# Keys of two batches loaded in packets of 768 bytes and turned in seven overlapping pieces per pair of heads

## The chip, the core and the metric

The kernel runs on one core of a Trainium2 chip. Its metric is the device time of one execution in microseconds (us). Three executions of the kernel before took 891.18, 894.32 and 895.53 us, so the median is 894.32 us. TensorE (PE) multiplies matrices and also turns (transposes) tiles by multiplying them with an identity matrix; its weight loads are listed apart as PEld. VectorE (DVE), ScalarE (ACT) and GpSimd (POOL) work on elements. SyncE (SP) issues most of the transfers (DMA) between the device's memory and the on-chip memory.

## The reference

Four batches of attention with twelve heads, 448 positions and 64 elements per head, with one 12x12 mix of the heads before the softmax and one after it, and behind it a gated feed-forward layer:

```python
scores = scale * np.matmul(q, k.transpose(0, 1, 3, 2))
scores = np.einsum('bhij,hg->bgij', scores, w_pre)
scores = scores - np.max(scores, axis=-1, keepdims=True)
attn = np.exp(scores)
attn = attn / (np.sum(attn, axis=-1, keepdims=True) + 1e-09)
attn = np.einsum('bhij,hg->bgij', attn, w_post)
attn_out = np.matmul(attn, v)
x = attn_out.transpose(0, 2, 1, 3).reshape(B * S, H * D)     # 1792 x 768
g = x @ w_gate                                                # 768 x 1536
out = (g / (1 + np.exp(-g)) * (x @ w_val)) @ w_out
```

## The kernel before

The work is a list of steps, each with a key (a number that says when it stands in the program). The steps are sorted by key and written out once, and each engine runs its own instructions in that order. Nothing is scheduled again on the chip: an instruction that waits holds up all that stands behind it on its engine, SP's transfers included.

Per batch, `load_k` brings the keys of a pair of heads. The first 384 positions are spread so that partition p holds positions 3p, 3p+1 and 3p+2. `load_k` puts the tile's columns in the order (position, head, element): three groups of 128 columns, each with 64 elements of the first head and 64 of the second. The 64 elements of one position and one head are a run of 256 bytes at both ends. The last 64 positions of all heads come in a transfer of their own (line 192 for batch 0, line 202 for the others). Batch 0's keys lie in one tile, and its loads are issued by SP and ACT in turn; batch 1 has a tile per pair, loaded by SP while batch 0 is computed.

`kprep` (line 228) turns a pair: three pieces of 128x128 and one for the last 64 positions (64x128) go to one bank of PE's output memory (`ktr`), and `kcopy` (lines 234 and 236) copies the bank to `kk`, with 64 partitions for each head. `qprep` and `qcopy` (lines 245, 252) do the same to the queries. `qk` (line 275) multiplies queries and keys, `qkcopy` (lines 284, 286) copies the scores to `stg`, and `store` (line 294) sends them to memory (`s_all`). `gather` (line 305) brings them back with positions and heads on the partitions (`rs`), `pre` (line 324) mixes the heads, `top` (335), `expo` (341) and `norm` (348 to 352) make the softmax, `post` (368) mixes again and turns, `mixed` (383) copies, and `av` (410) multiplies with the values (`vn`, loaded in lines 170 and 176). The feed-forward layer comes after batch 3, from about 400 us on.

At the start the order on PE is: 28 turns of the identity (line 218), queries, keys of pairs 0 and 1, queries, keys of pair 2, the first group of scores (`qk_0_0`, pairs 0 and 1), keys of pairs 3, 4 and 5, and the second and third group of scores. SP stores a group of scores, loads queries and values, stores the second and the third group, loads more values, and issues the first gathers. Batch 1's keys are turned one pair at a time between the `qk` and the `post` of one round of batch 0, from 65 to 89 us.

Of the kernel before, what the change touches and what calls it, by code (L numbers as in the profile page):

```python
# [24 lines left out]
def talking_heads_moe_kernel(ctx, tc, q, k, v, w_pre, w_post, w_gate, w_val, w_out, out):  # L25
    nc = tc.nc
    B, H, S, D = q.shape
    NT, DM = out.shape
    DFF = w_out.shape[0]
    P = 128  # L30
    TS = 10
    NC = -(-S // P)
    PART = S % P
# [64 lines left out]
    ident = cst.tile([P, P], F32, name="ident")  # L98
# [53 lines left out]
    qn, kn, vn, kk, qt, stg, rs, pts, sts, et, rw, ats, trs, qtrs, qks = ({} for _ in range(15))  # L152


    def keys(c):
        return min(P, S - c * P)
# [28 lines left out]
    def load_k(b, p, part=None, eng=nc.sync):  # L185
        full = S - PART
        n = (NC - 1) * 2 * D
        if b == 0:
            if "all" not in kn:
                kn["all"] = stp.tile([P, NPAIR * NC * 2 * D], F32, tag="stg", name="kn_0")  # L190
            if part == 1:
                eng.dma_start(
                    out=kn["all"][:PART, NPAIR * n:].rearrange("p (h d) -> p h d", d=D),
                    in_=k[b, :, full:].rearrange("h p d -> p h d"),
                )
                return
            t = kn["all"][:, p * n:(p + 1) * n]
            last = kn["all"][:PART, NPAIR * n + p * 2 * D:NPAIR * n + (p + 1) * 2 * D]
        else:
            if p == 0:  # L200
                kn["last"] = nat.tile([PART, H, D], F32, tag="kl", name=f"kl_{b}")
                nc.sync.dma_start(out=kn["last"], in_=k[b, :, full:].rearrange("h p d -> p h d"))
            t = nat.tile([P, n], F32, tag="kn", name=f"kn_{b}_{p}", bufs=6)
            last = kn["last"][:, 2 * p:2 * p + 2].rearrange("p h d -> p (h d)")
        eng.dma_start(
            out=t.rearrange("p (c j d) -> p (c j) d", j=2, d=D),
            in_=k[b, 2 * p:2 * p + 2, :full].rearrange("j (p c) d -> p c j d", c=NC - 1),
        )
        kn[b, p] = [t[:, c * 2 * D:(c + 1) * 2 * D] for c in range(NC - 1)] + [last]

    def first_act():
        t = smp.tile([P, 1], F32, tag="st", name="first_act", bufs=4)
# [7 lines left out]
    def kprep(b, p):  # L220
        kt = kn.pop((b, p))
        if b == 0:
            tr = ps.tile([P, S], F32, tag="pre" if p in (2, 3) else "post", name=f"ktr_{b}_{p}")
        else:
            tr = ps.tile([P, S], F32, tag="tr", bufs=2, name=f"ktr_{b}_{p}")
        for c in range(NC):
            m = keys(c)
            nc.tensor.transpose(tr[:, c * P:c * P + m], kt[c], ident[:m, :m])
        trs[b, p] = tr

    def kcopy(b, p):
# [234 lines left out]
    for b in range(B):  # L466
# [7 lines left out]
        if b == 0:  # L474
            at(-61.0, later(load_q, b, 0, nc.scalar))
            at(-60.9, first_act)
            at(-61.0, later(load_k, b, 0))
            at(-60.9, later(load_k, b, None, 1))
            for p in range(1, NPAIR):
                at(-60.8 + 0.01 * p, later(load_k, b, p, 0, nc.scalar if p % 2 else nc.sync))  # L480
# [3 lines left out]
            for i, (what, *a) in enumerate(order):  # L484
                n = -40.0 + i
                if what == "q":
                    at(n, later(qprep, b, *a))
                    at(n + 0.2, later(qcopy, b, *a))
                elif what == "k":
                    at(n, later(kprep, b, *a))  # L490
                    at(n + 0.2, later(kcopy, b, *a))
                else:
                    at(n, later(qk, b, *a))
                    for x in range(2):
                        at(n + 0.1, later(qkcopy, b, *a, x))
                    if a[0] == 0:
                        at(n + 0.6, later(store, b, *a, (nc.sync, nc.scalar)))
                    else:
                        at(n + 1.6, later(store, b, *a, (nc.sync, nc.scalar)))
        else:  # L500
            for p in range(NPAIR):
                n = slot(BACK - NUB - 4 + p)
                at(n0 - NTB + 0.4 + 0.01 * p if b > 1 and p < 3 else n - (9.3 if b > 1 else 4), later(load_k, b, p))
                at(n + 0.65, later(kprep, b, p))
                at(n + 0.8, later(kcopy, b, p))
# [396 lines left out]
    def gap(i, act=False):  # L902
        return (B - 1) * NTB + i // 2 * 2 + ((1.0, 1.84) if act else (0.7, 1.95))[i % 2]
# [4 lines left out]
    for b in range(NT // TB):  # L908
# [15 lines left out]
        for i in range(NFC):  # L924
            f = i // 2 + i % 2 * NFH if b else i
            n = n0 + i * T_F[b]
            if b:
# [19 lines left out]
                else:  # L947
                    last = f == NFC - 1
# [16 lines left out]
        if b:  # L965
            for i, (x, more, bq) in enumerate(AO):
                n = DOWN + i * NTC * T_Q
                for j in range(NFH // 2):
                    at_ff(n - 10.9 + 0.1 * j if i == 0 else n - 16 + j, later(b_load, i, j))
                    y, z = ((-6.6, -5.6), (-4.9, -3.9), (-1.6, -0.6))[j] if i == 0 else (3 * j - 12, 3 * j - 11)  # L970
                    at_ff(n + y, later(b_split, i, j, False))
                    at_ff(n + z, later(b_split, i, j, True))
                for c in range(NTC):
                    m = n + c * T_Q
# [25 lines left out]
        for n, u in units:  # L1000
            if unit_index(u) < EARLY:
# [4 lines left out]
                last = gap(FIRST + 5 * i + 5)  # L1006
# [13 lines left out]
            else:  # L1020
                d = n - LEAD
# [62 lines left out]
```

## Time and profile before

| what | value |
|---|---|
| median of three executions | 894.32 us (891.18 to 895.53) |
| the profiled execution, its own time | 898.02 us |
| its span, first to last instruction | 896.3 us |
| PE busy (matmuls) | 855.8 us, 95% of the span |
| DVE busy | 641.5 us, 72% |
| ACT busy | 457.9 us, 51% |
| DMA queue that SP issues to (q1) | 71.6% of 16 engines' span |

The profiled execution took 1.7 us more than its span and 3.7 us more than the median. An engine's busy time is an average over parts with different limits: from 400 us on PE has hardly a gap, while in the first 90 us it shares the time with transfers that keep all DMA engines busy. A row of the timeline gives start and length in us, the engine (a q behind it means that its sequencer issued a transfer), the line, the operation, output<-input, the shape and the count of instructions that were merged; in brackets stand the idle time of the engine ahead of the row and what ended it. "Issue" there means that the engine waited for nothing that the profile shows. A form such as 128*64 says rows * columns of the weights that PE holds; here that is the tile to be turned.

### The profile page before, as it was taken

The page shows a single profiled execution, that of the slowest core. Times are in us where ns is not written, and L with a number is a line of the kernel's source. Part 1 is how long each engine was busy: PE and PEld are TensorE (multiplying, and loading weights), DVE is VectorE, ACT ScalarE, POOL GpSimd, SP SyncE. Part 2 cuts the span into 40 slices and gives each one's busy share as a digit, 9 for nine tenths or more (in the row PEclk, how much of TensorE's full clock was granted, in tenths as well). Part 3 has the DMA queues.
Part 4 walks back from the last instruction along what each step waited for, and adds up shares of the span by engine and source line. Part 5 has one row for each costly group of instructions (what it writes and reads, how often), then busy time and mean ns, then how long its engine had stood idle before and what let it go on. Part 6 is the DMA issues. An engine that isn't in the chain of part 4 may idle for free.

```text
span 896.3 us, 26474 instructions
## 1 busy us (share of the span) xinstructions
PE 855.8 (95%) x10886; PEld 704.5 (79%) x10886; DVE 641.5 (72%) x1159; ACT 457.9 (51%) x1042; POOL 176.5 (20%) x255
## 2 busy tenths in 40 slices
PE   8688999999999898899999999999999999999998
PEld 5355666566656666678999999999999998999998
DVE  3565576656666666667989898678899979865853
ACT  3475677667766758644333334255554454353321
POOL 2111111111111112124545453111101121002020
PEclk9799999999999999999999999999999999999999
DMA  9998998989898859535998886446766579978696
GB/s 209 307 318 268 272 287 281 324 266 295 270 321 256 270 184 303 193 109 191 298 307 236 260 283 167 148 144 208 226 193 179 181 267 316 380 221 190 175 301 155
DMA packets 186033, 218.72 MB, mean 244 GB/s; under 512 B 58136, under 2 KB 153400, under 8 KB 185912
## 3 DMA queue, kind: packets, MB, share of 16 engines
q1 hardware_dynamic: 178856, 205.91, 71.6%
q0 software_dynamic: 3168, 8.26, 5.3%
q10 hardware_dynamic: 3888, 2.86, 1.2%
q8 instruction: 86, 1.41, 0.6%
q14 instruction: 35, 0.29, 0.1%
HBM read 138.15 MB, written 77.47 MB: 241 GB/s over the span
## 4 chain that ended last, share of the span: by engine, by line
PE 82%; DMA 7%; DVE 4%; ACT 3%; issue 3%; SPq 1%; ACTq 0%; DVEq 0%
PE av L410 8%; PE pre L324 8%; PE post L368 7%; PE p L713 6%; PE p L711 6%; PE p L710 6%; PE qk L275 5%; PE q L854 5%; PE q L853 5%; PE q L852 5%; PE upv L765 3%; PE upg L765 3%; PE upg L769 3%; PE upv L766 3%; PE upg L766 3%; PE upv L769 3%
## 5 line engine op out<-in xcount | busy, mean ns | idle before, releaser
L335 DVE TENSOR_REDUCE st<-pre 128x1 f32<-128x448 f32 x180 | 104.5, 620 | 79.9 <-PE pre L324 75.2
L341 ACT ACTIVATE e<-pre,st 128x448 f32<-128x448 f32 x180 | 112.8, 631 | 82.7 <-DVE st L335 76.2
L608 POOL TENSOR_SCALAR mag<-mag 128x768 f32<-128x768 f32 x33 | 100.6, 3050 | 258.3 <-ACT mag L606 258.3
L368 PEld LDWEIGHTS post<-rw,e 60*64 60x64 f32 x5040 | 97.5, 135 | 35.3 <-issue 28.4
L324 PE MATMUL pre<-rs,w_pre_blocks 64*64 64x448 f32 (+1 forms) x720 | 105.8, 564 | 15.9 <-DMA rs<-s_all 9.6
L352 POOL TENSOR_SCALAR rw<-w_post_gs,st 128x60 f32<-128x60 f32 x180 | 55.6, 323 | 331.0 <-DVE st L349 260.6
L368 PE MATMUL post<-rw,e 60*64 60x60 f32 x5040 | 104.3, 222 | 8.9 <-issue 7.1
L383 ACT ACTIVATE attnT<-post 128x420 f32<-128x420 f32 (+1 forms) x192 | 91.2, 541 | 20.6 <-PE post L368 19.8
L854 PE MATMUL q<-ohi,al 128*128 128x384 f32 x276 | 93.7, 339 | 1.3 <-DVE al L837 1.3
L410 PE MATMUL av<-attnT,vn 128*64 128x120 f32 (+9 forms) x1728 | 89.8, 264 | 5.2 <-issue 3.6
L852 PE MATMUL q<-ohi,ah 128*128 128x384 f32 x276 | 93.6, 339 | 1.0 <-ACT ah L845 1.0
L853 PE MATMUL q<-olo,ah 128*128 128x384 f32 x276 | 93.6, 339 | 0.0
L275 PE MATMUL qk<-kk,qt 64*64 64x448 f32 x672 | 92.6, 546 | 0.3 <-DVE w_post_gs L148 0.3
L410 PEld LDWEIGHTS av<-attnT,vn 128*64 128x64 f32 (+1 forms) x1728 | 71.0, 137 | 17.8 <-issue 9.3
L284 DVE COPY stg<-qk 128x448 f32<-128x448 f32 x120 | 71.1, 617 | 8.0 <-PE qk L275 4.7
L845 ACT ACTIVATE ah<-ar 128x768 fp32r<-128x768 f32 x46 | 38.6, 844 | 51.6 <-PE q L853 28.8
L275 PEld LDWEIGHTS qk<-kk,qt 64*64 64x64 f32 x672 | 31.8, 135 | 34.9 <-issue 23.3
L837 DVE TENSOR_TENSOR al<-ar,ah 128x768 fp32r<-128x768 f32 x46 | 43.9, 954 | 16.5 <-ACT ah L845 16.5
L854 PEld LDWEIGHTS q<-ohi,al 128*128 128x128 f32 x276 | 52.4, 190 | 1.9 <-DVE al L837 1.9
L852 PEld LDWEIGHTS q<-ohi,ah 128*128 128x128 f32 x276 | 52.3, 190 | 1.3 <-ACT ah L845 1.3
L765 PE MATMUL upv<-x,whi 128*128 128x448 f32 x144 | 53.2, 369 | 0.0
L765 PE MATMUL upg<-x,whi 128*128 128x448 f32 x144 | 53.2, 369 | 0.0
(141 smaller groups left out, 1656.7 us busy)
## 6 DMA issues: line engine op xcount, KB each, us to landing
rs<-s_all SPq DMA_DIRECT2D x88, 448.0 KB, 5.2
s_all<-stg SPq DMA_DIRECT2D x60, 448.0 KB, 4.9
w_d<-w SPq DMA_DIRECT2D x36, 384.0 KB, 4.6
raw<-in_moe_w_gate_dram SPq DMA_DIRECT2D x12, 768.0 KB, 5.3
raw<-in_moe_w_val_dram SPq DMA_DIRECT2D x12, 768.0 KB, 6.6
raw<-in_moe_w_out_dram SPq DMA_DIRECT2D x12, 768.0 KB, 5.9
w<-w_d SPq DMA_DIRECT2D x24, 384.0 KB, 5.9
s_all<-stg SPq DMA_DIRECT2D x39, 224.0 KB, 4.5
```

The costliest lines, as they stand in the source:

```text
L275: nc.tensor.matmul(pt[x][i * HB:(i + 1) * HB], qt[b, c][hs, p, r:r + HB], kk[b, p][hs], start=True, stop=True)
L324: nc.tensor.matmul(pt[r][x * HB:(x + 1) * HB], wpre[i], xs[i, x], start=True, stop=True)
L335: nc.vector.tensor_reduce(sts[b, u][:, 0, r:r + 1], pts[b, t], axis=AX.X, op=ALU.max, negate=True)
L341: nc.scalar.activation(e, pts.pop((b, t)), AF.Exp, bias=st[:, 0, r:r + 1], scale=1.0, accum_out=st[:, 1, r:r + 1])
L368: nc.tensor.matmul(ats[b, u][y][o * HB:(o + 1) * HB, to, :m], et[b, t][i, c * P + x * HB:c * P + (x + 1) * HB], rw[b, t][i, :, :m], start= ...
L383: nc.scalar.activation(attnT[:part, i, n0:n1, y * HS:y * HS + m], pt[:part, n0:n1, :m], AF.Copy)
L410: nc.tensor.matmul(o, vn[b][part, h, c], a, start=(c == 0 and x == 0), stop=(c == NC - 1 and x == 2 - m))
L608: eng.tensor_scalar(mag, mag, f32_of(0x38000000), f32_of(0x47EFFFFF), op0=ALU.max, op1=ALU.min)
L765: nc.tensor.matmul(pt, hi[:, c], xh[:, c, ts], start=(c == 0), stop=False)
L852: nc.tensor.matmul(pt, ahi, bhi, start=f == 0, stop=False)
L853: nc.tensor.matmul(pt, ahi, blo, start=False, stop=False)
L854: nc.tensor.matmul(pt, alo, bhi, start=False, stop=f == NFH - 1)
```

## The change

For batches 0 and 1 the keys' columns are laid out as (head, position, element), so that the three positions of one partition and one head are one run of 768 bytes at both ends of the transfer: 256 packets for a pair in place of 768. The two heads of one position are then no longer neighbours. A turn of columns 64(2+c) to 64(4+c) puts the second head's piece c on partitions 64 to 127 and something else on partitions 0 to 63; a second turn, of the 64 columns of the first head's piece c, writes over those 64 partitions. So a pair takes three turns of 128x128, three of 128x64 and the one for the last 64 positions: seven in place of four. Batches 2 and 3 keep their layout and their turns.

```diff
-        eng.dma_start(
-            out=t.rearrange("p (c j d) -> p (c j) d", j=2, d=D),
-            in_=k[b, 2 * p:2 * p + 2, :full].rearrange("j (p c) d -> p c j d", c=NC - 1),
-        )
-        kn[b, p] = [t[:, c * 2 * D:(c + 1) * 2 * D] for c in range(NC - 1)] + [last]
+        src = k[b, 2 * p:2 * p + 2, :full]
+        if b < 2:
+            eng.dma_start(
+                out=t.rearrange("p (j z) -> p j z", j=2), in_=src.rearrange("j (p c) d -> p j (c d)", c=NC - 1)
+            )
+        else:
+            eng.dma_start(
+                out=t.rearrange("p (c j d) -> p (c j) d", j=2, d=D), in_=src.rearrange("j (p c) d -> p c j d", c=NC - 1)
+            )
+        kn[b, p] = t, last
...
-        for c in range(NC):
-            m = keys(c)
-            nc.tensor.transpose(tr[:, c * P:c * P + m], kt[c], ident[:m, :m])
+        t, last = kt
+        for c in range(NC - 1):
+            to = slice(c * P, (c + 1) * P)
+            if b < 2:
+                nc.tensor.transpose(tr[:, to], t[:, (NC - 2 + c) * D:(NC + c) * D], ident)
+                nc.tensor.transpose(tr[:D, to], t[:, c * D:(c + 1) * D], ident)
+            else:
+                nc.tensor.transpose(tr[:, to], t[:, c * 2 * D:(c + 1) * 2 * D], ident)
+        nc.tensor.transpose(tr[:, (NC - 1) * P:], last, ident[:PART, :PART])
```

On PE at the start, before: the first queries (`qtr`) and the first two pairs of keys (`ktr`), with the shape of what is written.

```order
L245 MATMUL qtr_0_0_186<-ident,qn_0_115 128x64 x3
L228 MATMUL ktr_0_191<-ident,kn_117 128x128 x3
L228 MATMUL ktr_0_191<-ident,kn_117 128x64
L228 MATMUL ktr_1_198<-ident,kn_117 128x128 x3
L228 MATMUL ktr_1_198<-ident,kn_117 128x64
L245 MATMUL qtr_0_1_205<-ident,qn_0_115 128x64 x3
```

The same place in the changed kernel, up to the end of the first pair (lines are 11 higher behind the diff).

```order
L256 MATMUL qtr_0_0_186<-ident,qn_0_115 128x64 x3
L235 MATMUL ktr_0_191<-ident,kn_117 128x128
L236 MATMUL ktr_0_191<-ident,kn_117 64x128
L235 MATMUL ktr_0_191<-ident,kn_117 128x128
L236 MATMUL ktr_0_191<-ident,kn_117 64x128
L235 MATMUL ktr_0_191<-ident,kn_117 128x128
L236 MATMUL ktr_0_191<-ident,kn_117 64x128
L239 MATMUL ktr_0_191<-ident,kn_117 128x64
```

Nothing changed its place; three turns that stood in a row now alternate with three that write 64 partitions.

On SP at the start, before: the last key and query loads, the stores of the scores (`s_all<-stg`), the values, and the first gather.

```order
L205 DMA kn_117<-in_k_dram 128x6x64 x2
L183 DMA qn_1_127<-in_q_dram 128x12x64
L294 DMA s_all<-stg_0_0_223 64x896
L183 DMA qn_2_228<-in_q_dram 128x12x64
L176 DMA vn_230<-in_v_dram 64x12x64 x2
L294 DMA s_all<-stg_0_1_260 64x896
L170 DMA vn_230<-in_v_dram 128x3x192 x2
L294 DMA s_all<-stg_0_2_273 64x896
L170 DMA vn_230<-in_v_dram 128x3x192 x2
L305 DMA rs_0_286<-s_all 128x2x448
```

The same place in the changed kernel.

```order
L207 DMA kn_117<-in_k_dram 128x2x192 x2
L183 DMA qn_1_127<-in_q_dram 128x12x64
L305 DMA s_all<-stg_0_0_232 64x896
L183 DMA qn_2_237<-in_q_dram 128x12x64
L176 DMA vn_239<-in_v_dram 64x12x64 x2
L305 DMA s_all<-stg_0_1_278 64x896
L170 DMA vn_239<-in_v_dram 128x3x192 x2
L305 DMA s_all<-stg_0_2_291 64x896
L170 DMA vn_239<-in_v_dram 128x3x192 x2
L316 DMA rs_0_304<-s_all 128x2x448
```

The order stays; a key load has 2 runs of 192 elements per partition where it had 6 of 64.

On PE in batch 0's rounds, before: the second pair of batch 1's keys, between scores and the second mix.

```order
L275 MATMUL qk_3_3_1_1037<-kk_3_238,qt_3_765 64x448
L228 MATMUL ktr_1_1046<-ident,kn_1_886 128x128 x3
L228 MATMUL ktr_1_1046<-ident,kl_819 128x64
L245 MATMUL qtr_0_0_1052<-ident,qn_0_747 128x64 x3
L368 MATMUL post_9_0_1065<-rw_18_938,e_18_906 64x60 x2
```

The same place in the changed kernel.

```order
L286 MATMUL qk_3_3_1_1058<-kk_3_250,qt_3_783 64x448
L235 MATMUL ktr_1_1067<-ident,kn_1_904 128x128
L236 MATMUL ktr_1_1067<-ident,kn_1_904 64x128
L235 MATMUL ktr_1_1067<-ident,kn_1_904 128x128
L236 MATMUL ktr_1_1067<-ident,kn_1_904 64x128
L235 MATMUL ktr_1_1067<-ident,kn_1_904 128x128
L236 MATMUL ktr_1_1067<-ident,kn_1_904 64x128
L239 MATMUL ktr_1_1067<-ident,kl_837 128x64
L256 MATMUL qtr_0_0_1076<-ident,qn_0_765 128x64 x3
L379 MATMUL post_9_0_1089<-rw_18_956,e_18_924 64x60 x2
```

Here too three turns are added where one pair stands, and the neighbours keep their places.

## Rows read from the trace of the kernel before

**Rows 1.** The page: busy time of the engines, and all DMA packets by size.

```profile
PE 855.8 (95%) x10886; PEld 704.5 (79%) x10886; DVE 641.5 (72%) x1159; ACT 457.9 (51%) x1042; POOL 176.5 (20%) x255
...
DMA packets 186033, 218.72 MB, mean 244 GB/s; under 512 B 58136, under 2 KB 153400, under 8 KB 185912
```

**Rows 2.** The chain that ended last, first microseconds: start, length, what.

```profile
5.71 6.95 DMA kn<-in_k_dram
```

**Rows 3.** Timeline of PE and its weight loads, 6.5 to 16 us.

```profile
6.86 0.39 PE L245 MATMUL qtr<-ident,qn 64*128 64x64 f32 x3
7.18 1.43 PE L228 MATMUL ktr<-ident,kn 128*128 128x128 f32 x8
...
9.11 0.75 PE L228 MATMUL ktr<-ident,kn 128*128 128x128 f32 x4 [0.31 <-DMA kn<-in_k_dram]
...
9.58 0.14 PEld L228 LDWEIGHTS ktr<-ident,kn 64*128 64x128 f32 x1 [0.17 <-issue]
...
9.79 0.98 PE L275 MATMUL qk<-kk,qt 64*64 64x448 f32 x8
...
10.70 1.43 PE L228 MATMUL ktr<-ident,kn 128*128 128x128 f32 x8
...
12.79 0.72 PE L228 MATMUL ktr<-ident,kn 128*128 128x128 f32 x4 [0.66 <-DMA kn<-in_k_dram]
...
13.45 1.76 PE L275 MATMUL qk<-kk,qt 64*64 64x448 f32 x16
...
15.13 0.87 PE L245 MATMUL qtr<-ident,qn 128*128 128x128 f32 x6
```

**Rows 4.** Timeline of SP's stores and gathers and their neighbours, 11 to 30 us.

```profile
11.60 0.52 SPq L294 DMA_DIRECT2D s_all<-stg  x1
...
14.57 1.38 DVE L284 COPY stg<-qk 128x448 f32<-128x448 f32 x2 [0.40 <-PE qk L275]
...
16.15 0.82 SPq L294 DMA_DIRECT2D s_all<-stg  x1
...
19.10 0.50 SPq L294 DMA_DIRECT2D s_all<-stg  x1
...
24.25 1.43 SPq L305 DMA_DIRECT2D rs<-s_all  x3
...
29.65 1.77 PE L324 MATMUL pre<-rs,w_pre_blocks 64*64 64x448 f32 x8 [6.49 <-DMA rs<-s_all]
```

**Rows 5.** Timeline of PE at 398 us: from 128*128 to 128*64 weights.

```profile
398.18 0.36 PE L765 MATMUL upv<-x,whi 128*128 128x448 f32 x1
...
398.38 0.37 PE L766 MATMUL upv<-x,wlo 128*128 128x448 f32 x1
...
398.68 0.26 PE L410 MATMUL av<-attnT,vn 128*64 128x50 f32 x2
```

**Rows 6.** Timeline of PE, 64 to 78 us, where batch 1's keys are turned.

```profile
65.29 0.55 PE L228 MATMUL ktr<-ident,kn 128*128 128x128 f32 x3 [1.61 <-DMA kn<-in_k_dram]
...
71.58 0.97 PE L368 MATMUL post<-rw,e 60*64 60x60 f32 x50 [1.46 <-issue]
...
77.31 0.35 PE L368 MATMUL post<-rw,e 60*64 60x60 f32 x4 [1.35 <-issue]
```

**Rows 7.** Waits of PE over the span: total, times, longest, in us.

```profile
PE post L368 <- issue: 7.1, 6, 2.3
PE av L410 <- issue: 3.6, 2, 2.5
```

**Rows 8.** DMA packets of two stretches: 7 to 10 us, and 20 to 21.7 us.

```profile
DMA packets 2644, 0.65 MB, mean 217 GB/s; under 512 B 2644, under 2 KB 2644, under 8 KB 2644
...
DMA packets 624, 0.53 MB, mean 310 GB/s; under 512 B 25, under 2 KB 605, under 8 KB 623
```

**Rows 9.** Windows of the wait and of batch 1's keys: busy times, clock, DMA share, GB/s.

```profile
23.20:29.60 6.40, 0.00 (x0) 0.00 (x0) 0.62 (x1) 0.54 (x1) 0.00 (x0) 0.74 1.02 341
64.00:72.00 8.00, 5.25 (x119) 3.33 (x122) 5.21 (x14) 3.77 (x11) 0.77 (x3) 1.00 1.07 368
```

## The prediction

> **What bounds the kernel now.** I read the page first, then the chain of waits from the start, then the timeline around each place where keys are loaded or turned, and last the table of waits, the DMA packets and the windows. The page shows PE busy for 95% of the span [rows 1]: what is added to PE's program is paid unless it falls into one of PE's few gaps. The chain shows that the start is an exception: it runs through the last key load of batch 0, 5.71 to 12.66 us [rows 2]. So there are two places to price: the first 30 us, and 64 to 90 us, where batch 1's keys are turned while the DMA engines are fully busy (share 1.07 at 64 to 72 us [rows 9]). Behind that, PE's work is the same as before, and what was lost or won is carried to the end.
>
> In the start the reader is to see how little PE waits for keys: 0.31 us ahead of the third pair and 0.66 us ahead of the last [rows 3]. That is all that faster loads can give back before the first scores. Ahead of the first two pairs PE has no wait that a load ends.
>
> **What a turn costs.** Six equal turns in a row take 0.87 us with a last one of about 0.27 us, so one follows the other after (0.87 - 0.27) / 5 = 0.12 us. The piece for the last 64 positions, which stands alone between two other forms, starts at 9.58 us, and the next form at 9.79: 0.21 us. A pair of four turns takes 9.11 to 9.79 = 0.68 us [rows 3]. The trace has no turn of 128*64 weights. The nearest row for the change from 128*128 to 128*64 is at 398 us: the 128*128 matmuls follow each other after 0.20 us, the first 128*64 one comes 0.30 us after the last of them, so that change costs 0.10 us as well [rows 5]. I therefore price each of the seven pieces, all of them now between other forms, at 0.20 us: 7 x 0.20 = 1.40 us for a pair, 0.72 more than before. Twelve pairs make 8.6 us of PE time. The other end is that 128*64 and 128*128 follow each other like equal forms: 3 x 0.12 = 0.36 us more per pair, 4.3 in all. I take the upper end, since every change of form in these rows shows the gap.
>
> [...]
>
> **The start (batch 0).** The first pair starts at 7.18 us as before, since PE is then at the end of its queries, not waiting. Pairs 0 and 1 end 1.44 us later than before; the third pair then follows the queries without its wait of 0.31 us (three query turns and the change take 7.18 - 6.86 = 0.32), and the first scores start at 7.18 + 2.80 - 0.09 + 0.32 + 1.40 = 11.61 us where they started at 9.79: +1.8. (The 0.09 is that queries follow the 64-row piece without a change of form.) Scores take 10.70 - 9.79 = 0.91 us, then three pairs 4.20: the second scores start at 16.72 where they started at 13.45: +3.3. Faster loads have no part in these two: all keys are there by then.
>
> Behind them SP decides. Its first store of scores goes out at 11.60 us, and from there SP issues queries and values with hardly a pause up to the second store at 16.15 [rows 4]. It starts 1.8 us later, and would reach the second store at 17.97. That store also needs the copies of the second scores: the first of DVE's two copies ends at 14.57 + 0.69 = 15.26, now 18.5. So the second store goes 2.4 us later, at 18.55; the third store (19.10), the gathers that wait for it (24.25), and the first mix (29.65) follow by 2.4 us. Cover for this I see none: DVE, ACT and PE have no other work there. I take **+2.4 us**. The ends: with the low price of a turn the first scores are 3 x 0.36 - 0.31 = 0.8 us late and the second 6 x 0.36 - 0.97 = 1.2 late, which SP's queue turns into +0.8; if ACT's stores or the later scores set the start, it is the whole +3.3.
>
> **Batch 1.** Six pairs at 0.72 are 4.3 us on a PE that runs through from 65 to 89 us. Three things go against it. PE waits 1.61 us for the first pair [rows 6]. A pair's 197 KB take 0.91 us at 217 GB/s, the rate of packets that are all under 512 bytes, and 0.63 us at 310 GB/s, the rate of a stretch with mostly 768-byte ones [rows 8]: I take 0.3 us off the wait, with 0 and 1.6 as ends. [...] Next, PE stands still for 1.46 and 1.35 us inside `post` for its own instructions ("issue") just behind the second and third pair [rows 6]; if their arrival is set by the busy DMA engines, longer turns ahead of them are hidden there, up to 2 x 0.72. I take half, 0.7. Last, these two waits may themselves shorten with fewer packets, by 2.8 us at most; I take 0, since key packets are a small part of that traffic. That makes 4.3 - 0.3 - 0.7 = **+3.3 us**. Ends: +4.3, and below nothing with the low price of a turn and all waits gone, 2.2 - 1.6 - 2.8 = -2.2.
>
> No instruction is moved past another, no queue has more transfers, and no wait is added. The copies on DVE and ACT stay the same.
>
> **Sum.** The profiled execution took 898.0 us with its 1.7 us outside the span; 898.0 + 2.4 + 3.3 = 903.7. It was 3.7 us above the median of the runs, so the median is to be 894.3 + 5.7 = **900.0 us**. All ends together give -1.4 to +7.6.
>
> **Rivals.**
> No drain: forms alternate at 0.12 us. Start +0.8, batch 1 6 x 0.36 - 0.3 = +1.9: 897.0 us. Against it stand the gaps at every change of form.
> Swallowed: PE's wait of 6.49 us for the first gather [rows 4] is set by DMA engines at share 1.02 [rows 9], not by SP's order; then the start costs nothing, and both waits for instructions hide a whole pair's growth: 4.3 - 0.3 - 1.4 = +2.6, 896.9 us. Against it: the values that fill those engines are issued behind the delayed first store, so their load moves with it.
> Not slower: PE's instructions come through the same DMA engines. Its waits for them are 7.1 + 3.6 = 10.7 us over the span [rows 7], and 72 more matmuls and weight loads shift where each fetch falls in the program. If all of them went, and the 1.61 us too, that is 12.3 us against 2.4 + 4.3 = 6.7 added: 888.7 us. It decides the sign from the point where more than 6.7 of the 12.3 go. For it: two of these waits stand in the midst of the key loads. Against it: most of the 10.7 us lies where no key load changes, and a shift may add waits as well as take them.
> That the packets are not longer at all: the loads in a stretch of rows 8 that are laid out as the new ones appear as packets between 512 bytes and 2 KB, so I give it nothing.
>
> **Chances.** Forecast 0.58, with its own range of 897.8 to 901.9 (+3.5 to +7.6); no drain 0.12; swallowed 0.17; not slower 0.13. A measurement of this kernel can tell 0.5%, 4.5 us, from no change: 889.8 and 898.8. Of the forecast about 0.50 lies above 898.8 and 0.08 below it; no drain and swallowed are within; of the last case 0.12 is faster and 0.01 within. So slower 0.50, same 0.38, faster 0.12. The range of 8 in 10 reaches from 892.5, below the two small cases by the spread of runs, to 904.0, above the high end of 901.9 by the same.
>
> **What would show it.** Right: the first pair of keys takes 1.4 us on PE; the two scores start near 11.6 and 16.7 us, SP's third store near 21.5, the first mix near 32.1; from 65 us each pair takes 1.4; packets under 512 bytes fall by 12 x 768 to 48,920. Wrong: pairs of about 1.0 us; a first mix that stays at 29.7; or gaps ahead of `post` and `av` that sum to much less or more than 10.7 us, in which case the difference is in the fetching of instructions and not in the turns.

## The result, and the profile after

The changed kernel takes 902.09 us (median of six executions, 899.63 to 907.44); beside it on the same chip the kernel before took 892.75 us (890.52 to 898.85). The ratio is 1.0094 with a 95% interval of 1.0065 to 1.0123. So it is slower by about 8.4 us by that ratio (the two medians lie 9.3 us apart), with the forecast's sign, inside its range and 2.1 us above its 900.0. The traces and runs below show that the two terms of the sum make the smaller part of these 8.4 us.

One warning on the two profiles: that of before is a high execution of its kernel (898.02 us against medians of 893 to 897), that of after a low one (900.59 us against 902.09). They lie only 2.5 us apart. They can show how long a turn or a wait takes; the loss itself has to be read from repeated runs.

The page of the changed kernel, to be read against [rows 1], and the row of its instruction queue:

```profile
PE 861.4 (96%) x10922; PEld 708.3 (79%) x10922; DVE 643.8 (72%) x1159; ACT 458.1 (51%) x1042; POOL 176.3 (20%) x255
...
DMA packets 179889, 218.72 MB, mean 243 GB/s; under 512 B 48920, under 2 KB 147256, under 8 KB 179768
...
q8 instruction: 86, 1.41, 0.6%
```

The 36 added turns are there (10,922 matmuls for 10,886), and packets under 512 bytes fell to 48,920, as forecast. The last row (packets, MB, share of 16 engines) becomes important below.

The timeline of PE in the changed kernel at the first pairs, to be read against [rows 3]:

```profile
7.80 0.40 PE L256 MATMUL qtr<-ident,qn 64*128 64x64 f32 x3
8.13 0.33 PE L235 MATMUL ktr<-ident,kn 128*128 128x128 f32 x1
8.29 0.27 PE L236 MATMUL ktr<-ident,kn 128*64 128x128 f32 x1
8.40 0.27 PE L235 MATMUL ktr<-ident,kn 128*128 128x128 f32 x1
8.51 0.27 PE L236 MATMUL ktr<-ident,kn 128*64 128x128 f32 x1
8.62 0.27 PE L235 MATMUL ktr<-ident,kn 128*128 128x128 f32 x1
8.73 0.27 PE L236 MATMUL ktr<-ident,kn 128*64 128x128 f32 x1
8.93 0.27 PE L239 MATMUL ktr<-ident,kn 64*128 64x64 f32 x1
9.13 0.33 PE L235 MATMUL ktr<-ident,kn 128*128 128x128 f32 x1
...
11.33 0.98 PE L286 MATMUL qk<-kk,qt 64*64 64x448 f32 x8
```

Read the starts, not the lengths. From 8.29 on, turns of 128*128 and of 128*64 follow each other after 0.11 us whichever comes first. Only the 64*128 piece stands 0.20 us behind its forerunner, and the next pair 0.20 behind it. A pair takes 9.13 - 8.13 = 1.00 us, not 1.40. The queries started 0.94 us later than before, behind warm-up turns that took longer; that differs between executions (6.25 us in the profile of a kernel with the same added turns) and is no effect of the change.

SP's stores and gathers in the changed kernel, and the first mix, to be read against [rows 4]:

```profile
13.14 0.50 SPq L305 DMA_DIRECT2D s_all<-stg  x1
...
17.62 0.65 SPq L305 DMA_DIRECT2D s_all<-stg  x1
...
20.25 1.16 SPq L305 DMA_DIRECT2D s_all<-stg  x1
...
25.17 1.80 SPq L316 DMA_DIRECT2D rs<-s_all  x3
...
30.70 1.77 PE L335 MATMUL pre<-rs,w_pre_blocks 64*64 64x448 f32 x8 [5.89 <-DMA rs<-s_all]
```

The delay of 1.54 us at the first store shrinks to 1.05 at the first mix, which includes the later queries. One pair of profiles does not fix this delay: in the four profiles with seven turns in batch 0 (this one, after_again, b0_only, turns_only) the first mix starts at 30.70 to 31.85 us, in the four without them and without filler (before, packets_only, b1_only, turns_late) at 28.66 to 30.29, on average 1.8 us earlier.

The timeline of PE in batch 1, to be read against [rows 6]; first one more row of the kernel before, then the changed kernel:

```profile
61.61 0.50 PE L368 MATMUL post<-rw,e 60*64 60x60 f32 x17 [1.37 <-issue]
```

```profile
64.30 0.74 PE L379 MATMUL post<-rw,e 60*64 60x60 f32 x34 [2.15 <-issue]
...
67.26 0.47 PE L235 MATMUL ktr<-ident,kn 128*128 128x128 f32 x1
67.53 0.42 PE L236 MATMUL ktr<-ident,kn 128*64 128x128 f32 x1
67.74 0.42 PE L235 MATMUL ktr<-ident,kn 128*128 128x128 f32 x1
...
72.03 0.33 PE L235 MATMUL ktr<-ident,kn 128*128 128x128 f32 x1
```

The wait of 1.61 us for keys is gone, and so are the two waits of 1.46 and 1.35 us for instructions. A wait of 2.15 us for instructions stands ahead of the first pair; the kernel before has one in the same round of `post`, at 61.61 us, but of 1.37. The windows around the longer one (length; busy us of PE, PEld, DVE, ACT, POOL; granted clock; DMA share; GB/s):

```profile
62.00:64.20 2.20, 0.14 (x10) 0.01 (x2) 1.36 (x4) 0.73 (x4) 0.26 (x1) 1.00 1.10 311
64.30:66.00 1.70, 1.70 (x48) 1.30 (x52) 0.11 (x1) 0.83 (x2) 0.24 (x1) 0.93 1.11 279
66.00:67.00 1.00, 1.00 (x8) 0.00 (x0) 1.00 (x2) 0.57 (x2) 0.00 (x0) 0.50 1.04 396
67.00:69.00 2.00, 2.00 (x11) 1.19 (x7) 0.67 (x2) 1.38 (x5) 0.00 (x0) 0.50 1.06 377
69.00:70.00 1.00, 1.00 (x32) 0.81 (x35) 0.87 (x2) 0.00 (x0) 0.00 (x0) 0.92 1.02 393
```

PE stands still for two microseconds at a granted clock of 1.00, and then its clock is granted at 0.50, from about 66 to 69 us. The first pair's turns follow each other after 0.21 us there instead of 0.11. If it is the standing still that brings the lower clock, which these rows don't show by themselves, it was paid for twice here. Half the clock also stands behind other waits than those for instructions, and not behind each of these: fill36_turns and fill128_turns have the half clock from 69.1 and 68.3 us on behind waits of 3.3 and 2.55 us for keys, and the waits of 1.37 and 1.46 us of the kernel before have none behind them. Its wait of 1.35 us at 77 us is followed by half the clock:

```profile
76.00:78.00 2.00, 0.69 (x8) 0.43 (x11) 0.14 (x1) 0.39 (x1) 0.60 (x2) 0.87 1.05 266
78.00:80.00 2.00, 2.00 (x16) 0.63 (x8) 0.71 (x2) 0.61 (x2) 0.00 (x0) 0.50 0.97 254
80.00:82.00 2.00, 2.00 (x47) 1.14 (x46) 1.70 (x4) 1.34 (x4) 0.00 (x0) 0.78 0.02 4
```

Last, PE's waits for instructions over the span of the changed kernel (total, times, longest), to be read against [rows 7]:

```profile
PE post L379 <- issue: 7.5, 6, 2.2
PE pre L335 <- issue: 3.1, 2, 2.1
PE av L421 <- issue: 2.2, 3, 1.3
```

They sum to 12.8 us. Before they were 10.7 in `post` and `av`, and 11.4 with 0.7 ahead of `pre`, a row that [rows 7] leaves out. The sum changed little, but most of the places did.

### The profile page after: what moved, and what is told of

Same layout as the page of the kernel before. It is cut to its first block, busy times and chain, and to the rows that moved or that the text cites. A ratio compares the mean times of both kernels' runs of the same rounds, so it can differ in the third digit from the quotient of the medians.

```text
span 898.8 us, 26546 instructions
## 1 busy us (share of the span) xinstructions
PE 861.4 (96%) x10922; PEld 708.3 (79%) x10922; DVE 643.8 (72%) x1159; ACT 458.1 (51%) x1042; POOL 176.3 (20%) x255
## 2 busy tenths in 40 slices
DMA packets 179889, 218.72 MB, mean 243 GB/s; under 512 B 48920, under 2 KB 147256, under 8 KB 179768
## 3 DMA queue, kind: packets, MB, share of 16 engines
q8 instruction: 86, 1.41, 0.6%
## 4 chain that ended last, share of the span: by engine, by line
PE 82%; DVE 7%; DMA 4%; issue 4%; ACT 3%; SPq 0%; POOL 0%; ACTq 0%; DVEq 0%; POOLq 0%
PE pre L335 9%; PE post L379 8%; PE av L421 8%; PE qk L286 6%; PE p L724 6%; PE p L722 6%; PE p L721 6%; PE q L865 4%; PE q L864 4%; PE q L863 4%; PE upv L777 3%; PE upv L776 3%; PE upv L780 3%; PE upg L780 3%; PE upg L776 3%
## 5 line engine op out<-in xcount | busy, mean ns | idle before, releaser
L335 PE MATMUL pre<-rs,w_pre_blocks 64*64 64x448 f32 (+1 forms) x720 | 108.1, 561 | 14.1 <-DMA rs<-s_all 9.0
L617 ACT ACTIVATE mag<-raw 128x768 f32<-128x768 f32 x36 | 32.8, 911 | 41.7 <-DVE w L631 29.7
L777 PE MATMUL upv<-x,wlo 128*128 128x448 f32 x144 | 52.9, 367 | 0.7 <-DVE wlo L647 0.7
```

What stands on the lines that cost most here:

```text
L335: nc.tensor.matmul(pt[r][x * HB:(x + 1) * HB], wpre[i], xs[i, x], start=True, stop=True)
L777: nc.tensor.matmul(pt, lo[:, c], xh[:, c, ts], start=False, stop=False)
```

## The experiments

All were timed beside the kernel before on the same chip, in four groups. Its medians in these were 895.09, 896.02, 895.17 and 896.54 us, so 0.1% is 0.9 us.

| kernel | added PE instructions | median, us | ratio to before [95%] |
|---|---|---|---|
| packets_only | 0 | 895.21 | 1.0016 [0.9990, 1.0042] |
| turns_only | 72 | 908.45 | 1.0147 [1.0109, 1.0186] |
| before_fill36 | 144, idle time | 895.84 | 1.0016 [0.9988, 1.0044] |
| before_fill128 | 512, past idle time | 913.99 | 1.0220 [1.0196, 1.0244] |
| after_again (as changed) | 72 | 904.70 | 1.0111 [1.0063, 1.0158] |
| b0_only | 36 | 905.71 | 1.0106 [1.0069, 1.0143] |
| b1_only | 36 | 904.10 | 1.0085 [1.0056, 1.0114] |
| turns_late | 72, batches 2 and 3 | 901.82 | 1.0060 [1.0033, 1.0087] |
| fill36_turns | 72, idle time | 902.89 | 1.0091 [1.0061, 1.0120] |
| fill18_turns | 36, idle time | 902.57 | 1.0077 [1.0046, 1.0108] |
| after_fill92 | 72 + 184 in idle time | 897.42 | 1.0034 [1.0004, 1.0064] |
| fill128_turns | 256, idle time | 894.79 | 0.9982 [0.9955, 1.0010] |

A matmul and its weight load count as two instructions.

**The halves apart: packets_only and turns_only.** The first loads in packets of 768 bytes and turns the columns as they then lie, in four turns; the keys of batches 0 and 1 are therefore in another order. The second loads as before and adds a second turn of 64 columns, which writes again what the first wrote.

```diff
 # packets_only, against the changed kernel
-            if b < 2:
-                nc.tensor.transpose(tr[:, to], t[:, (NC - 2 + c) * D:(NC + c) * D], ident)
-                nc.tensor.transpose(tr[:D, to], t[:, c * D:(c + 1) * D], ident)
-            else:
-                nc.tensor.transpose(tr[:, to], t[:, c * 2 * D:(c + 1) * 2 * D], ident)
+            nc.tensor.transpose(tr[:, to], t[:, c * 2 * D:(c + 1) * 2 * D], ident)
 # turns_only, against the kernel before
             nc.tensor.transpose(tr[:, c * P:c * P + m], kt[c], ident[:m, :m])
+            if b < 2 and c < NC - 1:
+                nc.tensor.transpose(tr[:D, c * P:(c + 1) * P], kt[c][:, :D], ident)
```

> Keys of batches 0 and 1 in packets of 768 bytes, but four turns per pair as before, of the columns as they stand (so batches 0 and 1 get their keys' columns in another arrangement; nothing else is left out). PE's program has as many instructions as before. Supply theory (the loss comes from where PE's instruction fetches fall in its program, and up to 85 us the change is even a gain): the seven turns cost 12 x 0.33 = 4.0 us, and in the changed kernel's profile PE is 0.7 us ahead at 85 us, so the packets alone give 4 to 5 us: ratio 0.995. Turns theory (the added turns are the cost, packets give next to nothing): ratio 1.000, within 1 us. Packet theory (the longer packets themselves slow the start or other transfers): above 1.003.

> Keys in packets of 256 bytes as before, but seven turns per pair in batches 0 and 1 (the added turn writes the same 64 partitions again). PE's program has the same instructions as the changed kernel. Turns theory: 12 x 0.33 = 4.0 us, ratio 1.0045, and first scores about 1 us later. Supply theory: the same 4.0 us and the same unlucky fetch positions as the changed kernel, without the gain from packets: 9 to 13 us, ratio 1.010 to 1.015. Packet theory: ratio 1.000 to 1.004, below the changed kernel's 1.009.

The longer packets alone give nothing that can be measured. The turns alone cost 13 us, more than the 12 x 0.33 = 4 us of PE time that they take. So there is a cost of the turns that is not their own duration.

**Moving PE's program in idle time: before_fill36 and before_fill128.** Small plain matmuls of a constant are put into PE's wait for the first gather (6.49 us, [rows 4]).

```diff
+    def fill():
+        t = ps.tile([P, S], F32, tag="post", name="fill")
+        for _ in range(FILL):
+            nc.tensor.matmul(t[:D, :16], ident[:D, :D], ident[:D, :16], start=True, stop=True)
...
+    at(-21.0, fill)
```

> The kernel before, with 36 small matmuls (64x64 weights, 16 columns, output unused) put where PE waits for the first gather, 23 to 29.6 us. They add as many instructions to PE's program as the changed kernel's 36 turns (72 with their weight loads) and no time outside that wait. Supply theory: later fetches fall where they fall in the changed kernel, +4 to +8 us, ratio 1.004 to 1.009. Turns theory: no change, 0.998 to 1.002. If the small matmuls keep PE's granted clock from falling to 0.5 at 26 to 36 us, both shift by up to -3 us, which the clock in the profile and the next kernel show.

> As the kernel with 36 small matmuls, but 128 of them, 256 instructions, which is one whole fetch of 16 KB: later fetches fall at the same instructions as in the kernel before. Supply theory: no change but for the clock, 0.997 to 1.002, and at least 4 us faster than with 36. Turns theory: the same as with 36. If both are equally fast or slow against the kernel before, the position of fetches is not the cause.

Both missed their purpose. One such matmul shows as two in the trace, each with a weight load (before_fill36 has 10,958 matmuls and as many weight loads for 10,886), so 36 of them add 144 instructions and not 72. The 128 add 512, and they overran the wait:

```profile
22.68 23.40 PE L224 MATMUL fill<-ident 64*64 64x16 f32 x255
```

That puts the first mix at 45.8 us instead of 29.7, which is 16 of the 20 us lost; nothing on the position can be read from its time. What stays is that a move by 144 instructions shows no loss (at most 0.44%, where its interval ends).

**The batches apart and the turns elsewhere: after_again, b0_only, b1_only, turns_late.** The same kernel again; packets and turns in one batch only (`if b < 1`, `if b == 1` in place of `if b < 2`); and the added turns in batches 2 and 3, with the loads as before.

```diff
 # turns_late, against the kernel before
+            if b >= 2 and c < NC - 1:
+                nc.tensor.transpose(tr[:D, c * P:(c + 1) * P], kt[c][:, :D], ident)
```

> The changed kernel once more, beside the kernel before on this chip, for a second profile and the granted clock of each execution. Clock theory (the added turns take 12 x 0.33 = 4.0 us of PE, and the rest of the loss is PE's granted clock, which is lower on average, 0.985 against 0.988 in the executions so far, because PE waits in other places): ratio 1.006 to 1.012, mean clock 0.984 to 0.986, and time without the loss at half clock 4 to 5 us above the kernel before's. Turns theory (nothing but the turns' time): 1.0045 and the same clock as before.

> The change for batch 0 alone (long packets and seven turns); batch 1 as before. Clock theory: the first mix 1.0 us later as in the changed kernel's profile, ratio 1.001 to 1.004, clock at 0.986 to 0.988. Start theory (the order of SP's stores and loads behind the late first scores carries the loss): most of the changed kernel's loss, 1.006 to 1.010.

> The change for batch 1 alone; batch 0 as before. Clock theory: 6 x 0.33 = 2.0 us of turns between 65 and 90 us and a clock somewhat lower, ratio 1.003 to 1.007. Start theory: at most the 2.0 us of turns, less what the packets give, 0.999 to 1.002.

> All loads as before, and the three added turns per pair (written over the same 64 partitions) in batches 2 and 3 in place of 0 and 1: the same 36 turns, where batch 0's start and batch 1's key loads aren't touched. Clock theory: 4.0 us of turns plus what the clock loses; if turns lower the clock wherever they stand, 1.010 to 1.015 as in the kernel that has them in batches 0 and 1 with short packets (1.0147); if it is the waits of the first 90 us, 1.003 to 1.006 with the clock at 0.987 to 0.989. Turns theory: 1.0045.

The loss is confirmed. Each half of the change costs nearly as much as the whole: 1.06% and 0.85% against 0.94 and 1.11%. A cost per turn would have given two halves that add up. Something is lost as soon as some turns stand there, in whichever batch. turns_late lost 0.60% (0.33 to 0.87); that is within reach of the 0.45% of its turns alone, so it decides nothing.

**The decisive set: idle-time turns.** The same turns of 64 columns of the identity, 64*128, 0.066 us apart, stand in PE's wait for the first gather. Keys, their packets and their turns are untouched in all but after_fill92, which is the changed kernel with 92 of them, so that 72 + 184 = 256 instructions are added. fill128_turns has 106 in that wait and 22 in the next one, 256 instructions in all.

```diff
+    def fill():
+        t = ps.tile([P, S], F32, tag="post", name="fill")
+        for _ in range(FILL):      # 36, 18, 92; or 106 and 22
+            nc.tensor.transpose(t[:, :D], ident[:D], ident[:D, :D])
...
+    at(-21.0, fill)
```

> The kernel before, with 36 turns of a 64x128 tile (64 columns, output unused, 0.06 us each) where PE waits for the first gather. The small matmuls of the earlier filler runs turned out as two matmuls each in the trace (10958 against 10886 for 36 of them), so that kernel moved PE's program by 144 instructions, not by 72; a turn is one. This one moves it by 72, as the changed kernel does behind its last added turn. Position theory (PE stands still when one of its fetches of 256 instructions, and where each falls in the program decides how long): slower by at least 4 us though no work is added outside a wait, ratio 1.004 to 1.010, clock 0.984 to 0.986. Turns theory (added turns cost, wherever the fetches fall): 0.998 to 1.002, clock 0.987 to 0.988.

> The same with 18 turns, 36 instructions, as much as the change for one batch alone moves the program. Position theory: 1.004 to 1.009, near the 1.0085 and 1.0106 of the kernels with the change in one batch less their 2 us of turns. Turns theory: 0.998 to 1.002.

> The changed kernel with 92 such turns in the same wait (24.8 to 30.7 us in its profile), 184 instructions: behind batch 1's last added turn the program is 256 instructions on, one whole fetch, so that later fetches fall as in the kernel before. 92 x 0.06 = 5.6 us of the wait's 5.9. Position theory: only the start and the turns are left, 2 to 4 us, ratio 1.002 to 1.005, 4 us faster than the changed kernel. Turns theory: 1.009 to 1.011 as the changed kernel, or more if the first mix comes later.

> The kernel before with 128 turns of a constant tile (64x128 of the identity, results not used), 256 instructions: 106 of them in PE's wait for the first gather, 22 in its wait ahead of the second mix. Keys and their turns as before. 92 such turns took 6.03 us, so 106 take 6.9 us against a wait of 6.5 and 22 take 1.4 against 1.46: at most 0.5 us of PE time is added. Theory position: 256 instructions are a whole fetch, PE's program behind 33 us stands against the fetches as in the kernel before, so the ratio is 1.000 to 1.003, below that of 36 and of 18 turns (1.0091, 1.0077). Rival, turns in idle time cost by themselves (by the clock, or by whatever else they leave behind them) in proportion: 128 / 36 x 0.9% = 3%, and at the least the 1.009 of 36 turns.

36 turns in idle time cost 0.91%, as much as the whole change, though they take 2.5 us out of a wait that lasts longer. 128 of them cost nothing. So it is not the number of turns that counts, but by how many instructions the program behind them is moved: 36 and 72 hurt, 256 does not, nor did the 144 above. The timelines of both, fill36_turns first, up to the scores that stand among the first mixes (`qk`, line 281 and line 280):

```profile
22.95 2.48 PE L224 MATMUL fill<-ident 64*128 64x64 f32 x36
30.11 1.77 PE L330 MATMUL pre<-rs,w_pre_blocks 64*64 64x448 f32 x8 [4.67 <-DMA rs<-s_all]
...
38.50 0.96 PE L281 MATMUL qk<-kk,qt 64*64 64x448 f32 x8
```

```profile
23.01 6.91 PE L223 MATMUL fill<-ident 64*128 64x64 f32 x106
30.48 1.60 PE L329 MATMUL pre<-rs,w_pre_blocks 64*64 64x448 f32 x8 [0.56 <-DMA rs<-s_all]
32.01 2.60 PE L223 MATMUL fill<-ident 64*128 64x64 f32 x22
...
39.26 0.98 PE L280 MATMUL qk<-kk,qt 64*64 64x448 f32 x8
```

With 128 turns PE reaches this point 0.76 us later than with 36, so what the turns do to the clock or to the transfers up to here is no gain. From there on both run the same instructions, and yet the first ends at 901.1 us and the second at 893.6. Waits for instructions in the first, and then in the second:

```profile
PE post L374 <- issue: 9.3, 10, 2.2
...
PE av L416 <- issue: 2.0, 4, 0.8
...
PE pre L330 <- issue: 1.2, 1, 1.2
```

```profile
PE post L373 <- issue: 4.5, 5, 1.4
...
PE av L415 <- issue: 3.0, 3, 2.1
```

That is 12.5 us in 15 waits against 7.5 in 8. after_fill92 has 8.6 us in its profile and takes back two thirds of the loss: 1.0034 against 1.0094 and 1.0111.

Why 256? The row of the instruction queue above gives 1.41 MB in 86 packets, 16.4 KB each, for 21,844 matmuls and weight loads: one packet for 254 of them. In fill128_turns the row has one packet more:

```profile
q8 instruction: 87, 1.43, 0.7%
```

Four waits of the changed kernel for instructions (ending at 336.61, 344.02, 351.25 and 358.56 us) each stand 252 matmuls and weight loads behind the one before, counted by their starts; three of the kernel before (61.61, 71.58 and 77.31 us) 250 and 252. So PE's program comes in pieces of about 250 to 254 of these instructions. That 256 is a whole piece, so that a move by 256 puts every later piece's start before the same instruction as in the kernel before, is the author's estimate from these numbers.

The traces show these pieces at work. In the 14 profiles PE has 124 waits for "issue" of more than 0.3 us, and each of them ends 1.2 to 1.9 us after a packet of q8 (16,384 bytes) has landed. In the changed kernel, for example, PE stands still from 342.10 to 344.02 us, and a packet of q8 takes from 341.69 to 342.57. The places follow the position, too. Of the changed kernel's ten such waits and the eleven of fill36_turns, both 72 instructions on, seven stand behind the same number of matmuls and weight loads, ahead of the same instruction. Three of them, the changed kernel first:

```profile
344.02 0.51 PE L379 MATMUL post<-rw,e 60*64 60x60 f32 x20 [1.92 <-issue]
...
351.25 0.61 PE L379 MATMUL post<-rw,e 60*64 60x60 f32 x25 [1.54 <-issue]
...
358.56 0.59 PE L335 MATMUL pre<-rs,w_pre_blocks 60*64 60x448 f32 x2 [2.09 <-issue]
```

```profile
344.13 0.51 PE L374 MATMUL post<-rw,e 60*64 60x60 f32 x20 [1.37 <-issue]
...
351.44 0.61 PE L374 MATMUL post<-rw,e 60*64 60x60 f32 x25 [2.22 <-issue]
...
358.99 0.59 PE L330 MATMUL pre<-rs,w_pre_blocks 60*64 60x448 f32 x2 [1.17 <-issue]
```

Of the eight of fill128_turns four stand ahead of an instruction where the kernel before waits too, 256 later in the count. Two of them, the kernel before first:

```profile
312.14 0.33 PE L368 MATMUL post<-rw,e 60*64 60x60 f32 x4 [2.26 <-issue]
...
362.33 1.41 PE L410 MATMUL av<-attnT,vn 128*64 128x120 f32 x24 [2.50 <-issue]
```

```profile
310.55 0.33 PE L373 MATMUL post<-rw,e 60*64 60x60 f32 x4 [1.39 <-issue]
...
360.53 1.41 PE L415 MATMUL av<-attnT,vn 128*64 128x120 f32 x24 [2.06 <-issue]
```

## Why the prediction was right, and where it was not

The sign and the size came out. The reason that the forecast gave was not the one.

**The price of a turn** is the step that failed: "each of the seven pieces, all of them now between other forms, at 0.20 us". It measured 0.11 us between 128*128 and 128*64, in both orders and in all pairs at full clock, and 0.20 only at the 64*128 piece. The low end of the bound, 0.36 us more per pair, was right (0.33 measured); twelve pairs cost 4.0 us, not 8.6. The row it was read from [rows 5] changes its matmul's line and operands along with the form, and was too far away. The trace of the changed kernel shows no gap between these two forms (0.11 us against 0.12 for equal ones). Of the rivals, "no drain", by which the forms alternate at 0.12 us, had this step right.

**The start** was to lose 2.4 us at the first mix; the profile of the changed kernel shows 1.05, with queries that were 0.94 us late for another reason, and the eight profiles above some 1.8. So the size was not far off. The first scores, though, were 1.54 us late with those queries, 0.6 of it by the turns, where the forecast had 1.8; the low price had 0.8.

**Batch 1** was to lose 3.3 us. Its pairs took 1.00 us at full clock; the wait for keys went wholly and not by 0.3 us; the two instruction waits went wholly, and the one ahead of the first pair, which the forecast had not counted, grew from 1.37 to 2.15 us. That the packets shortened the wait for keys isn't shown: it varies between profiles and was 3.3 us with unchanged loads in fill36_turns, and packets_only won nothing in the end.

**What was missing** is the term that makes most of the loss: about 8 us for moving PE's program by 72 instructions (fill36_turns 0.91%, 95% interval 0.61 to 1.20). The "not slower" rival named the mechanism word for word, "72 more matmuls and weight loads shift where each fetch falls in the program", and gave it the wrong sign; its counter-argument, that "a shift may add waits as well as take them", was the truth. What the change costs apart from that is what after_fill92 leaves, 0.34% or 3 us (0.4 to 5.7), in place of the sum's 5.7. The two add up to 11 us, more than the 8.4 of the first measurement and the 9.9 of after_again, but within the intervals. So the time came out near 900 by luck: a term about twice too big stood in for one that was missing. Gaps ahead of `post` and `av` with another sum were named as a sign of this, but one profile of each kernel is no test of it: 10.7 before and 9.7 after, while the executions of one kernel lie up to 13 us apart (889.87 to 902.93).

**What stays open.** Why 36 and 72 instructions hurt, and 144 and 256 don't, is not settled: the traces show that PE waits for late pieces, not why a piece is late at one place and in time at another. The sum of instruction waits in one profile does not order the kernels: fill18_turns had 14.7 us in a profiled execution of 896.6, at a granted clock of 0.992, turns_only 9.9 in one of 901.2. One stretch does. From 335 to 372 us these waits sum to 5.8 to 7.3 us in the eight profiles of kernels moved by 36 or 72 instructions, and to 2.2 to 4.1 in the other six. The stretch was picked after looking, and the difference is only 2 to 5 us. The granted clock goes with the loss only in part (means 0.988 before, 0.985 after, 0.981 turns_only, 0.986 fill36_turns, 0.993 fill128_turns). It doesn't explain the loss, since before_fill36 lost nothing measurable at 0.987; but fill128_turns, at 0.993, may owe some of its time to the clock and not to its position. And of the 8.3 us by which fill36_turns and fill128_turns part behind those scores, 4.4 have come together at 409 us, where the attention ends for PE, and waits for instructions can account for them (5.0 more in fill36_turns); the other 3.9 arise in the feed-forward layer, where neither profile shows such a wait, and aren't taken apart. turns_only lost 0.4 to 0.5% more than the changed kernel, with overlapping intervals; whether the packets give that back isn't shown.

## What to carry to other kernels

Here, on an engine busy for 95% of the span, instructions added early in idle time cost up to 0.9% (36 turns, 72 instructions), more than the work added, and nothing measurable with 128 turns (256 instructions); the author puts that down to where the pieces of its program begin. Before a loss or gain of this size is put down to an edit, move the unchanged program by the same number of instructions in idle time, and the edited one to a whole piece. Price a change of matmul form from rows with the same pair of forms, or carry both ends through.

## What the runs showed that was not expected

- TensorE turned 128*128 and 128*64 tiles alternately at 0.11 us each, no slower than equal forms (0.12 us, [rows 3]).
- PE's program arrives in packets of 16.4 KB, one for some 254 matmuls and weight loads; PE waits up to 3.0 us at a few of them, above all in `post`, each time until 1.2 to 1.9 us after the packet has landed; in the two places shown a wait of 1.35 to 2.15 us was followed by about 3 us at granted clock 0.50.
- A plain matmul of 64x64 weights and 16 columns in this data type shows as two matmuls with a weight load each (36 added 72 to the 10,886 matmuls); a turn shows as one (36 added 36).
- The program moved by 256 instructions ran at a mean granted clock of 0.993, where the kernel before had 0.988 on the same chip, at no measurable change of time.
